# Threshold attention and a gated FFN on one core: the first weights fetched between the first operands, ScalarE's table loaded at once, one unsplit job, and two VectorE operations laid over separate columns

## The chip, the cores and the metric

The kernel runs on one core of one Trainium2 chip. The metric is the device time of one execution in microseconds: the median of the runs shown. Before the change it is 1088.98 us over 3 runs (1088.27 to 1091.62). A core has five engines that run their own instruction streams in order and wait for each other by semaphores: TensorE (PE, with PEld for its weight loads), VectorE (DVE), ScalarE (ACT), GpSimd (POOL) and SyncE (SP), which here issues every DMA.

## The reference

Eight batches, eight heads, 576 positions, head dimension 64. Attention keeps only the scores within tau of their row's maximum. Its output, heads side by side (512 wide), goes through a mixing step with the position before, and then through a feed-forward part with a squared ReLU and a sigmoid gate.

```python
scores = scale * np.matmul(q, k.transpose(0, 1, 3, 2))
thresh = np.max(scores, axis=-1, keepdims=True) - tau
scores = np.where(scores >= thresh, scores, -1000000000.0)
attn = np.exp(scores - np.max(scores, axis=-1, keepdims=True))
attn = attn / (np.sum(attn, axis=-1, keepdims=True) + 1e-09)
x = np.matmul(attn, v)                  # then heads side by side: (8, 576, 512)
x_prev = np.concatenate([np.zeros((B, 1, D)), x[:, :-1, :]], axis=1)
xk = mu_k * x + (1.0 - mu_k) * x_prev
xr = mu_r * x + (1.0 - mu_r) * x_prev
k = np.maximum(xk @ w_k, 0.0)           # w_k: 512 x 1024
v = k * k @ w_v                         # w_v: 1024 x 512
r = 1.0 / (1.0 + np.exp(-(xr @ w_r)))   # w_r: 512 x 512
out = r * v
```

## The kernel before

**Jobs and units.** A job is one pair of heads of one batch. It fetches its operands (`raw`: queries and keys, and `v`), scales the queries on ScalarE (line 427, which needs a factor made from tau by two small VectorE operations, lines 295 and 303), and goes through units of 128 query rows for both heads, and one unit for the last 64 rows. A job is either *plain*, and multiplies the operands as they are (line 530), or *split*: ScalarE rounds them to a high half (line 448), GpSimd subtracts to get the low half (line 458, in two pieces), eight DMAs stack the halves into `st` tiles (line 477), and the scores are products of stacked halves (line 541). The number of plain jobs at the start is `PLAIN`, 2 here.

**The softmax of a unit.** For each head: the maximum (VectorE, line 575), the threshold (ScalarE, line 583), the exponential (ScalarE, line 591), and mask and sum in one (VectorE, line 599). Then, for both heads at once, an addition to the two sums and a reciprocal (VectorE, lines 609 and 610). GpSimd scales the rows (line 624), the TensorE transposes them (line 648), ScalarE or VectorE empties the PSUM (lines 666 and 668), and the TensorE multiplies by the values (line 728). The small numbers of a unit live in `sm`, a tile of 4 kinds by 2 heads, so the two sums lie in neighbouring columns.

**The weights.** All three weight matrices arrive as 64-bit words, in 20 pieces of 128 x 512 (8 of w_k, 4 of w_r, 8 of w_v). Each piece is rebuilt as a 32-bit number in `xT[1]`, which serves as a scratch tile until the second batch needs it: absolute value (ScalarE, line 353), clamp (VectorE, line 361), mask and shift (VectorE, line 375), sign and low bits from the words (VectorE, lines 382 and 392, with two SBUF inputs), then rounding (ScalarE, line 399) and the rest (GpSimd, line 403). So each piece costs the VectorE four operations.

**The feed-forward part.** It runs in chunks of 256 positions: differences (GpSimd, line 821), mixing (VectorE, line 830), rounding and rest (lines 843 and 851), products with w_k (line 873), w_r (line 915) and w_v (line 937).

**What sets the order.** No engine's order is written by hand. Each step is entered with its engine, an assumed duration, its inputs and outputs, and a key; a list scheduler (`Plan.order`) then takes, on each engine, the step that can start first by its own assumed clock, and the lower key among equals. DMAs are one engine of this plan, so the order in which SyncE issues them comes out of it too. A weight's fetch has a key and an earliest time (`wait`); `W0` to `W3` set those times: 3.0 us and then every 3.5 us for the eight pieces of w_k, from 50 us on every 2 us for the other twelve. The order is fixed when the program is built.

Of the kernel before, what the change touches and what calls it, by code (L numbers as in the profile page):

```python
# [8 lines left out]
F32 = mybir.dt.float32  # L9
FR = mybir.dt.float32r  # L10
AF = mybir.ActivationFunctionType
ALU = mybir.AluOpType
# [4 lines left out]
W_MIN = 2.0 ** (0x38 * 2 - 127)  # L17
W_MAX = 2.0 ** (0x8F - 127) * (1 + 0x6FFFFF / 2.0**23)
# [199 lines left out]
def tile_threshold_attention_then_rwkv_ffn(  # L218
# [14 lines left out]
    V, A, G, PE, SY = nc.vector, nc.scalar, nc.gpsimd, nc.tensor, nc.sync  # L233
# [4 lines left out]
    P = 128  # L238
# [22 lines left out]
    add = plan.add  # L261
    DQ = 0.55
    HALF = 2
    W0, W1, W2, W3, AVK = 3.0, 3.5, 50.0, 2.0, 4.5
    PREP, PB, VB, COLD, EARLY = 8, 2, 2, 24, 30
    EV = ("ACT", 0.49), ("DVE", 0.6)
    KMAX, KEXP, KMASK = 0.0, 0.0, 0.5
# [1 line left out]
    def sbuf(tag, shape, dtype=F32, bufs=1):  # L269
        return plan.buf(sb, tag, shape, dtype, bufs)  # L270

    def psum(tag, shape, bufs):
        return plan.buf(ps, tag, shape, F32, bufs)

    def fixed(name, shape, dtype=F32):
        return plan.buf(const, name, shape, dtype, make=lambda: const.tile(shape, dtype, name=name))
# [7 lines left out]
    small = fixed("small", [P, 4])  # L284
# [2 lines left out]
        0.06,  # L287
        lambda: SY.dma_start(small.get()[:, 0:1], tau.rearrange("(o t) -> o t", o=1).broadcast_to([P, 1])),
        writes=[(small, 0)],
        key=-100,  # L290
    )
    add(
        "DVE",
# [2 lines left out]
        reads=[(small, 0)],  # L296
        writes=[(small, 1)],
        key=-100,
# [5 lines left out]
        reads=[(small, 0)],  # L304
        writes=[(small, 2)],
        key=-100,
# [5 lines left out]
    xT = [fixed(f"xT{j}", [P, NCT, SM + 1]) for j in range(2)]  # L312
# [2 lines left out]
    xE = fixed("xE", [P, NCT, NE, ST + 1])  # L315


    bd = fixed("bd", [P, 2, P], FR)
    add("DVE", 0.3, lambda: V.memset(bd.get().bitcast(F32), 0.0), writes=[bd], key=-99)

# [5 lines left out]

    pieces = {}

    def weight(j, name, w, c, f, key, wait):
        plan.soft = True  # L330
        tag = f"w{name}{c}{f}"
        words = sbuf(tag, [P, 512, 2], U32)
        piece = sbuf(tag, [P, 2, 512], FR)
        pieces[name, c, f] = piece
        col = j % 4
        box = (xT[1], (col, 0)), (xT[1], (col, 1))

        def t():
            return xT[1].get()[:, col, 1 : 1 + 512]

        add(
            "DMA",
            DQ,
            lambda: SY.dma_start(words.get().rearrange("p n w -> p (n w)").bitcast(I64), w[c, f]),
            writes=[words],
            key=key - 6,
            kb=512,
            wait=wait,
        )
        add(  # L350
            "ACT",
            0.56,
            lambda: A.activation(t(), words.get()[:, :, 1].bitcast(F32), AF.Abs),
            reads=[words],
            writes=box,
            key=key,
        )
        add(
            "DVE",
            0.55,  # L360
            lambda: V.tensor_scalar(t(), t(), W_MIN, W_MAX, op0=ALU.max, op1=ALU.min),
            writes=box,
            key=key,
        )

        def u():
            return t().bitcast(U32)

        def word(y):
            return words.get()[:, :, y]  # L370

        add(
            "DVE",
            0.55,
            lambda: V.tensor_scalar(u(), u(), 0x07FFFFFF, 3, op0=ALU.bitwise_and, op1=ALU.logical_shift_left),
            writes=box,
            key=key,
        )
        add(
            "DVE",  # L380
            0.85,
            lambda: V.scalar_tensor_tensor(  # L382
                u(), word(1), 0xC0000000, u(), op0=ALU.bitwise_and, op1=ALU.bitwise_or
            ),
            reads=[words],
            writes=box,
            key=key,
        )
        add(
            "DVE",  # L390
            0.85,
            lambda: V.scalar_tensor_tensor(  # L392
                u(), word(0), 29, u(), op0=ALU.logical_shift_right, op1=ALU.bitwise_or
            ),
            reads=[words],
            writes=box,
            key=key,
        )
        add("ACT", 0.53, lambda: A.activation(piece.get()[:, 0], t(), AF.Copy), reads=box, writes=[(piece, 0)], key=key)
        add(  # L400
            "POOL",
            1.27,
            lambda: G.tensor_tensor(piece.get()[:, 1], t(), piece.get()[:, 0].bitcast(F32), op=ALU.subtract),
            reads=[(piece, 0), *box],
            writes=[(piece, 1)],
            key=key,
        )
        plan.soft = False
# [142 lines left out]
    def softmax(unit):  # L551
        n = unit["n"]
        ys = (0, 1) if unit["kind"] == "P" else (1,)

        sm = sbuf("sm", [P, 4, 2], F32, 4)
        p = unit["p"] = sbuf("p", [P, 2, S], F32, PB)
        ss = {y: psum("s", [P, 2, 512], 2) for y in ys}
        scores(unit, ss, float(n))
        for y in ys:
            key = float(n + (y if len(ys) == 2 else 0))  # L560
            s = ss[y]

            def sv(s=s):
                return s.get()[:, :, 0:HS]

            def pv(y=y):
                return p.get()[:, y].rearrange("p (a b) -> p a b", a=2)

            def col(j, y=y):
                return sm.get()[:, j, y : y + 1]  # L570

            add(
                "DVE",
                0.67,
                lambda sv=sv, col=col: V.tensor_reduce(col(0), sv(), axis=AX.XY, op=ALU.max, negate=True),  # L575
                reads=[s],
                writes=[(sm, (0, y))],
                key=key - KMAX,
            )
            add(  # L580
                "ACT",
                0.186,
                lambda col=col: A.activation(col(1), col(0), AF.Identity, bias=small.get()[:, 1:2], scale=-1.0),  # L583
                reads=[(sm, (0, y)), (small, 1)],
                writes=[(sm, (1, y))],
                key=key - KEXP,
            )
            add(
                "ACT",
                0.625,  # L590
                lambda sv=sv, pv=pv, col=col: A.activation(pv(), sv(), AF.Exp, bias=col(0)),  # L591
                reads=[s, (sm, (0, y))],
                writes=[(p, y)],
                key=key - KEXP,
            )
            add(
                "DVE",
                0.74,
                lambda sv=sv, pv=pv, col=col: V.scalar_tensor_tensor(  # L599
                    pv(), sv(), col(1), pv(), op0=ALU.is_ge, op1=ALU.mult, accum_out=col(2)  # L600
                ),
                reads=[s, (sm, (1, y))],
                writes=[(p, y), (sm, (2, y))],
                key=key - KMASK,
            )
        ysl = slice(ys[0], 2)

        def invert():
            V.tensor_scalar(sm.get()[:, 2, ysl], sm.get()[:, 2, ysl], 1e-9, None, op0=ALU.add)  # L609
            V.reciprocal(sm.get()[:, 3, ysl], sm.get()[:, 2, ysl])  # L610

        add(
            "DVE",
            0.33,
            invert,
            reads=[(sm, (2, y)) for y in ys],
            writes=[(sm, (3, y)) for y in ys],
            key=n + 0.5,
        )
        for y in ys:  # L620
            add(
                "POOL",
                0.715,
                lambda y=y: G.tensor_scalar(  # L624
                    p.get()[:, y], p.get()[:, y], sm.get()[:, 3, y : y + 1], 0.0, op0=ALU.mult, op1=ALU.add
                ),
                reads=[(sm, (3, y))],
                writes=[(p, y)],
                key=n - 1.0,
            )  # L630
# [329 lines left out]


    halved = {j: ([0, 1], [2, "T", 3]) for j in range(HALF)}
    PLAIN = 2
    jobs = []
    n = 0
    for b in range(B):
        for part, order in enumerate(halved.get(b, (["T", 0, 1, 2, 3],))):
            for hp in range(NPAIR):
                job = dict(ji=len(jobs), b=b, hp=hp, first=n, groups={}, plain=len(jobs) < PLAIN, units=[])
                job.update(tail="T" in order, tg=int(part == 1), src=qk, nq=S, c0=0)  # L970
# [8 lines left out]
    wlist = [  # L979
        (name, w, c, f)  # L980
        for name, w in (("k", w_k), ("r", w_r), ("v", w_v))
        for f in range(w.shape[1])
        for c in range(w.shape[0])
    ]
    wfr = [W0 + W1 * j if j < 8 else W2 + W3 * (j - 8) for j in range(len(wlist))]
    wat = [2.0 + 2.0 * j for j in range(len(wlist))]

    operands(jobs[0], -1.0)
    add("DMA", DQ, lambda: SY.dma_start(mu_sb.get(), mu.rearrange("p (j c) -> p j c", j=2)), writes=[mu_sb], key=0.0)
    for j, (name, w, c, f) in enumerate(wlist):  # L990
        weight(j, name, w, c, f, wat[j], wfr[j])
    for job in jobs:
        if job["ji"] + 1 < len(jobs):
            operands(jobs[job["ji"] + 1], float(jobs[job["ji"] + 1]["first"]))
        b, seen = job["b"], set()
# [9 lines left out]
        if job["hp"] == NPAIR - 1:  # L1005
            key = unit["n"] - 30.0
# [60 lines left out]
```

## Time and profile before

| what | value |
|---|---|
| median of 3 runs | 1088.98 us |
| the profiled execution | 1088.13 us |
| its span, first to last instruction | 1086.3 us |
| mean granted TensorE clock | 0.986 |
| PE busy | 1019.4 us (94%) |
| DVE busy | 777.1 us (72%) |
| ACT busy | 736.4 us (68%) |
| POOL busy | 581.6 us (54%) |
| chain that ended last, by engine | PE 74%, DVE 15%, ACT 4%, DMA 2% |

The page divides the span into 40 slices of 27 us and shows each engine's busy share in tenths. The shares over the whole span mix two stages, so they are read slice by slice. A group's line gives count, busy time in us, mean duration in ns, and then the engine's idle time before it with what ended it. A matrix product's end is modelled, so a busy TensorE need not be one at its peak.

### The profile page before, as it was taken

The page shows a single profiled execution, that of the slowest core. Times are in us where ns is not written, and L with a number is a line of the kernel's source. Part 1 is how long each engine was busy: PE and PEld are TensorE (multiplying, and loading weights), DVE is VectorE, ACT ScalarE, POOL GpSimd, SP SyncE. Part 2 cuts the span into 40 slices and gives each one's busy share as a digit, 9 for nine tenths or more (in the row PEclk, how much of TensorE's full clock was granted, in tenths as well). Part 3 has the DMA queues.
Part 4 walks back from the last instruction along what each step waited for, and adds up shares of the span by engine and source line. Part 5 has one row for each costly group of instructions (what it writes and reads, how often), then busy time and mean ns, then how long its engine had stood idle before and what let it go on. Part 6 is the DMA issues. An engine that isn't in the chain of part 4 may idle for free.

```text
span 1086.3 us, 19493 instructions
## 1 busy us (share of the span) xinstructions
PE 1019.4 (94%) x6832; PEld 842.7 (78%) x6832; DVE 777.1 (72%) x1707; ACT 736.4 (68%) x1556; POOL 581.6 (54%) x590
## 2 busy tenths in 40 slices
PE   4666899999999999999999999999999999999998
PEld 2444766888888887888887878886889788888887
DVE  6999999779887788777877877766878498222220
ACT  4776876787867777687777767865777667344442
POOL 3666776556645556556455554573555445344441
PEclk8888999999999999999999999999999999999999
DMA  6784467556445344453544434541545041000000
GB/s 217 197 304 108 115 171 188 131 159 182 110 117 127 100 109 113 112 130 96 125 115 104 105 98 114 119 96 50 137 105 128 25 100 35 21 20 20 20 21 19
DMA packets 44351, 118.44 MB, mean 109 GB/s; under 512 B 7392, under 2 KB 10976, under 8 KB 44256
## 3 DMA queue, kind: packets, MB, share of 16 engines
q1 hardware_dynamic: 44256, 117.21, 41.4%
q8 instruction: 55, 0.90, 0.3%
q14 instruction: 40, 0.33, 0.1%
HBM read 46.14 MB, written 9.44 MB: 51 GB/s over the span
## 4 chain that ended last, share of the span: by engine, by line
PE 74%; DVE 15%; ACT 4%; DMA 2%; issue 2%; SPq 1%; POOL 1%; POOLq 0%; ACTq 0%; DVEq 0%
PE w L873 17%; PE w L937 15%; PE w L728 12%; PE s L541 10%; PE w L648 10%; PE w L915 8%; DVE p L599 4%; DVE sm L575 3%; DVE mk L830 2%; PE s L516 2%; ACT p L591 1%; DVE sm L609 1%; DVE xT L392 1%; DVE xT L382 1%; DMA st<-lo 1%
## 5 line engine op out<-in xcount | busy, mean ns | idle before, releaser
L624 POOL TENSOR_SCALAR p<-p,sm 128x576 f32<-128x576 f32 x288 | 226.8, 798 | 222.8 <-DVE sm L610 160.3
L599 DVE SCALAR_TENSOR_TENSOR p<-s,sm,p 128x576 f32<-128x576 f32 x288 | 232.2, 813 | 59.4 <-ACT p L591 55.9
L873 PE MATMUL w<-xk,wk 128*128 128x256 f32 x1728 | 233.8, 284 | 0.0
L575 DVE TENSOR_REDUCE sm<-s 128x1 f32<-128x576 f32 x288 | 210.8, 749 | 31.5 <-PE s L541 21.3
L937 PE MATMUL w<-wv,k 128*128 128x512 f32 x864 | 220.9, 396 | 0.9 <-ACT pm L666 0.9
L648 PE MATMUL w<-ident,p 128*128 128x128 f32 x1312 | 197.0, 282 | 24.9 <-POOL p L624 23.6
L873 PEld LDWEIGHTS w<-xk,wk 128*128 128x128 f32 x1728 | 217.6, 189 | 1.7 <-issue 0.5
L591 ACT ACTIVATE p<-s,sm 128x576 f32<-128x576 f32 x288 | 209.8, 730 | 0.4
L648 PEld LDWEIGHTS w<-ident,p 128*128 128x128 f32 x1312 | 154.0, 144 | 67.1 <-POOL p L624 44.2
L937 PEld LDWEIGHTS w<-wv,k 128*128 128x128 f32 x864 | 155.5, 188 | 28.7 <-ACT pm L666 1.4
L851 POOL TENSOR_TENSOR xk<-mk,xk 128x512 fp32r<-128x512 f32 x72 | 93.2, 1294 | 112.4 <-ACT xk L843 112.2
L583 ACT ACTIVATE sm<-sm,small 128x1 f32<-128x1 f32 x288 | 83.6, 290 | 100.0 <-DVE sm L575 92.9
L666 ACT ACTIVATE pm<-w 128x512 f32<-128x512 f32 x174 | 102.5, 591 | 69.9 <-PE w L648 69.0
L728 PE MATMUL w<-pm,v 128*64 128x256 f32 (+1 forms) x1024 | 142.7, 414 | 2.4 <-DVE pm L668 1.9
L830 DVE SCALAR_TENSOR_TENSOR mk<-m,mu_sb,xT 128x256 f32<-128x256 f32 x128 | 84.1, 697 | 73.0 <-POOL xk L851 73.0
L541 PE MATMUL s<-st 128*128 128x288 f32 x496 | 116.5, 316 | 17.6 <-issue 8.7
L896 POOL TENSOR_TENSOR k<-r,k 128x512 fp32r<-128x512 f32 x72 | 93.7, 1303 | 72.9 <-ACT k L886 69.0
L458 POOL TENSOR_TENSOR lo<-raw,hi 128x576 fp32r<-128x576 f32 (+2 forms) x76 | 106.8, 1422 | 39.9 <-ACT hi L448 38.9
L728 PEld LDWEIGHTS w<-pm,v 128*64 128x64 f32 x1024 | 69.6, 137 | 55.7 <-issue 8.6
L915 PE MATMUL w<-wr,xk 128*128 128x512 f32 x432 | 110.4, 396 | 0.0
L541 PE MATMUL s<-st,st 128*128 128x288 f32 x496 | 109.0, 301 | 0.0
L541 PEld LDWEIGHTS s<-st 128*128 128x128 f32 x496 | 79.6, 191 | 37.6 <-issue 20.4
(62 smaller groups left out, 1125.0 us busy)
## 6 DMA issues: line engine op xcount, KB each, us to landing
raw<-in_qk SPq DMA_DIRECT2D x24, 608.0 KB, 4.8
st<-hi SPq DMA_DIRECT2D x48, 304.0 KB, 3.2
st<-lo SPq DMA_DIRECT2D x48, 304.0 KB, 4.0
v<-in_v SPq DMA_DIRECT2D x40, 320.0 KB, 3.9
out<-sg SPq DMA_DIRECT2D x32, 256.0 KB, 2.0
st<-hi SPq DMA_DIRECT2D x48, 144.0 KB, 3.4
st<-lo SPq DMA_DIRECT2D x48, 144.0 KB, 3.8
wk<-in_w_k SPq DMA_DIRECT2D x8, 512.0 KB, 5.9
```

The source lines that it names most:

```text
L458: lambda cs=cs: G.tensor_tensor(lo.get()[:, cs], raw.get()[:, cs], hi.get()[:, cs].bitcast(F32), op=ALU.subtract),
L541: PE.matmul(ss[y].get()[:, z, 0:HS], l.get()[:, c * P : (c + 1) * P], r.get()[:, keys(y, z)], start=(j == 0), stop=(j == 1),)
L575: lambda sv=sv, col=col: V.tensor_reduce(col(0), sv(), axis=AX.XY, op=ALU.max, negate=True),
L591: lambda sv=sv, pv=pv, col=col: A.activation(pv(), sv(), AF.Exp, bias=col(0)),
L599: lambda sv=sv, pv=pv, col=col: V.scalar_tensor_tensor(pv(), sv(), col(1), pv(), op0=ALU.is_ge, op1=ALU.mult, accum_out=col(2)),
L624: lambda y=y: G.tensor_scalar(p.get()[:, y], p.get()[:, y], sm.get()[:, 3, y : y + 1], 0.0, op0=ALU.mult, op1=ALU.add),
L648: PE.transpose(pt.get()[:, c, :], p.get().rearrange("p y s -> p (y s)")[:, o : o + P], ident.get())
L728: PE.matmul(o.get()[hs, 0:n], vt.get()[:, c, hs], pt[:, 0:n], start=(c == 0), stop=(c == 4))
L830: V.scalar_tensor_tensor(d.get()[:, y, o : o + n], diff.get()[:, y, o : o + n], mu_sb.get()[:, j, hc + y : hc + y + 1], prv[:, hc + y], op ...
L873: PE.matmul(h.get()[:, f], l, r, start=(ct == 0 and i == 0), stop=(ct == NCT - 1 and i == 2))
L915: PE.matmul(z.get(), l, r, start=(ct == 0 and i == 0), stop=(ct == NCT - 1 and i == 2))
L937: PE.matmul(vps.get(), l, r, start=(ft == 0 and i == 0), stop=(ft == NFT - 1 and i == 2))
```

## The change

Six edits. Tau is fetched second, behind the first job's operands. A one-column exponential of a zero is added at ScalarE's start, which brings its table load there. The first two weights are fetched between the first operands, and the fetch times become 1.5 us apart for w_k and 1 us apart for the rest. `PLAIN` is 1. The two one-input operations of the weight conversion go over the same 512 columns in another order: column 0, column 256, column 1, column 257 and so on. And `sm` is turned round, so that the two sums lie four columns apart.

```diff
-    W0, W1, W2, W3, AVK = 3.0, 3.5, 50.0, 2.0, 4.5
+    W0, W1, W2, W3, AVK = 3.0, 1.5, 50.0, 1.0, 4.5
...
         lambda: SY.dma_start(small.get()[:, 0:1], tau.rearrange("(o t) -> o t", o=1).broadcast_to([P, 1])),
         writes=[(small, 0)],
-        key=-100,
+        key=-13.9,
...
+    add(
+        "ACT",
+        1.5,
+        lambda: A.activation(small.get()[:, 3:4], xT[0].get()[:, 0, 0:1], AF.Exp),
+        reads=[(xT[0], "zero")],
+        writes=[(small, 3)],
+        key=-99,
+    )
...
+        def far(x):
+            return x.rearrange("p (a b) -> p b a", a=2)
...
             lambda: SY.dma_start(words.get().rearrange("p n w -> p (n w)").bitcast(I64), w[c, f]),
             writes=[words],
-            key=key - 6,
+            key=fetch,
             kb=512,
-            wait=wait,
+            wait=max(wait, 0.0),
...
-            lambda: V.tensor_scalar(t(), t(), W_MIN, W_MAX, op0=ALU.max, op1=ALU.min),
+            lambda: V.tensor_scalar(far(t()), far(t()), W_MIN, W_MAX, op0=ALU.max, op1=ALU.min),
...
-            lambda: V.tensor_scalar(u(), u(), 0x07FFFFFF, 3, op0=ALU.bitwise_and, op1=ALU.logical_shift_left),
+            lambda: V.tensor_scalar(far(u()), far(u()), 0x07FFFFFF, 3, op0=ALU.bitwise_and, op1=ALU.logical_shift_left),
...
-        sm = sbuf("sm", [P, 4, 2], F32, 4)
+        sm = sbuf("sm", [P, 2, 4], F32, 4)
...
             def col(j, y=y):
-                return sm.get()[:, j, y : y + 1]
+                return sm.get()[:, y, j : j + 1]
...
-            V.tensor_scalar(sm.get()[:, 2, ysl], sm.get()[:, 2, ysl], 1e-9, None, op0=ALU.add)
-            V.reciprocal(sm.get()[:, 3, ysl], sm.get()[:, 2, ysl])
+            V.tensor_scalar(sm.get()[:, ysl, 2], sm.get()[:, ysl, 2], 1e-9, None, op0=ALU.add)
+            V.reciprocal(sm.get()[:, ysl, 3], sm.get()[:, ysl, 2])
...
-    PLAIN = 2
+    PLAIN = 1
...
-    wfr = [W0 + W1 * j if j < 8 else W2 + W3 * (j - 8) for j in range(len(wlist))]
+    wfr = [W0 + W1 * (j - 2) if j < 8 else W2 + W3 * (j - 8) for j in range(len(wlist))]
     wat = [2.0 + 2.0 * j for j in range(len(wlist))]
+    wfe = [-13.0, -8.5, *(w - 6.0 for w in wat[2:])]
...
-        weight(j, name, w, c, f, wat[j], wfr[j])
+        weight(j, name, w, c, f, wat[j], wfe[j], wfr[j])
```

The plan's order comes out differently nearly everywhere, most of all in the first 130 us. Two places follow; line numbers of the changed kernel are 14 higher from line 344 on (16 at the end), and the number behind a tile's name only tells one buffer from another.

The VectorE's first operations before, from the two that prepare tau's factors (line 295) to the first piece of a weight that is taken up (`xT`, with `wk` the words it is made of); `s` are scores, `p` the exponentials:

```order
L303 TENSOR_SCALAR small<-small 128x1
L575 TENSOR_REDUCE sm_103<-s_94 128x1
L575 TENSOR_REDUCE sm_103<-s_96 128x1
L599 SCALAR_TENSOR_TENSOR p_107,sm_103<-s_94,sm_103,p_107 128x576
L599 SCALAR_TENSOR_TENSOR p_107,sm_103<-s_96,sm_103,p_107 128x576
L609 TENSOR_SCALAR sm_103<-sm_103 128x2
L610 RECIPROCAL sm_103<-sm_103 128x2
L361 TENSOR_SCALAR xT_77<-xT_77 128x512
L375 TENSOR_SCALAR xT_77<-xT_77 128x512
```

The same place now:

```order
L303 TENSOR_SCALAR small<-small 128x1
L375 TENSOR_SCALAR xT_75<-xT_75 128x256x2
L389 TENSOR_SCALAR xT_75<-xT_75 128x256x2
L589 TENSOR_REDUCE sm_117<-s_101 128x1
L589 TENSOR_REDUCE sm_117<-s_103 128x1
L396 SCALAR_TENSOR_TENSOR xT_75<-wk_0_82,xT_75 128x512
L613 SCALAR_TENSOR_TENSOR p_125,sm_117<-s_101,sm_117,p_125 128x576
L613 SCALAR_TENSOR_TENSOR p_125,sm_117<-s_103,sm_117,p_125 128x576
L623 TENSOR_SCALAR sm_117<-sm_117 128x2
L624 RECIPROCAL sm_117<-sm_117 128x2
```

Two operations of the first weight stand ahead of the first maximum and a third ahead of the first mask, where before no weight was touched until the first unit's softmax was through.

SyncE's first DMAs before (`small` is tau, `raw` an operand of queries and keys, `v` the values, `wk` a weight):

```order
L288 DMA small<-in_tau 128x1
L419 DMA raw_75<-in_qa 128x896
L419 DMA raw_81<-in_qa 128x896
L436 DMA v_83<-in_v 128x640
L436 DMA v_85<-in_v 128x640
L989 DMA mu_sb<-in_mu 128x8
L344 DMA wk_0_89<-in_w_k 128x512
L344 DMA wk_0_101<-in_w_k 128x512
L344 DMA wk_0_112<-in_w_k 128x512
L344 DMA wk_0_130<-in_w_k 128x512
```

And now:

```order
L433 DMA raw_71<-in_qa 128x896
L288 DMA small<-in_tau 128x1
L358 DMA wk_0_82<-in_w_k 128x512
L433 DMA raw_84<-in_qa 128x896
L358 DMA wk_0_86<-in_w_k 128x512
L450 DMA v_88<-in_v 128x640
L450 DMA v_90<-in_v 128x640
L1005 DMA mu_sb<-in_mu 128x8
L358 DMA wk_0_94<-in_w_k 128x512
L358 DMA wk_0_98<-in_w_k 128x512
```

The first operand passed tau, one weight stands between the two operands and one behind them. Three more weights follow, and only then the first stacked halves, which are those of the second job.

More of the change, by code (lines that the diff above doesn't have):

```diff
@@ L327, in tile_threshold_attention_then_rwkv_ffn, with weight @@
     pieces = {}
-    def weight(j, name, w, c, f, key, wait):
+    def weight(j, name, w, c, f, key, fetch, wait):
         plan.soft = True
@@ L624, in softmax @@
                 lambda y=y: G.tensor_scalar(
-                    p.get()[:, y], p.get()[:, y], sm.get()[:, 3, y : y + 1], 0.0, op0=ALU.mult, op1=ALU.add
+                    p.get()[:, y], p.get()[:, y], sm.get()[:, y, 3:4], 0.0, op0=ALU.mult, op1=ALU.add
                 ),
```

## The prediction

> **What bounds the kernel now.** I read the page's forty slices first, then sums of busy time by stretch, then the groups of the stretch that stood out.
>
> ```profile
> span 1086.3 us, 19493 instructions
> ...
> PE   4666899999999999999999999999999999999998
> ...
> DVE  6999999779887788777877877766878498222220
> ...
> PEclk8888999999999999999999999999999999999999
> ```
>
> One slice is 27 us. From the sixth on the TensorE is busy 90% or more; before that it is not, and there it is the VectorE that shows nines. So there are two stages, and a change of the first 130 us must be priced on the VectorE. The sums by stretch say how hard that bound is (columns: stretch, its length, then PE, PEld, DVE, ACT and POOL busy, granted clock, DMA share):
>
> ```profile
> 0.00:10.00 10.00, 2.29 (x8) 1.19 (x8) 1.03 (x6) 2.19 (x3) 0.70 (x6) 1.00 0.74 265
> 10.00:101.00 91.00, 56.20 (x292) 37.94 (x293) 88.46 (x157) 59.83 (x129) 55.30 (x48) 0.83 0.67 205
> 101.00:163.00 62.00, 56.22 (x367) 43.12 (x367) 57.46 (x119) 52.56 (x113) 46.07 (x44) 1.00 0.56 144
> 163.00:1086.00 923.00, 904.70 (x6169) 760.45 (x6168) 630.19 (x1429) 621.82 (x1312) 479.56 (x493) 1.00 0.38 96
> ```
>
> From 10 to 101 us the VectorE works 88.46 of 91 us while the TensorE idles 34.8. A microsecond of VectorE time saved there is close to a microsecond of the span. From 163 us on the TensorE idles 18.3 of 923, and VectorE time is worth little. The groups of the VectorE in the first 101 us (count, busy us, mean ns):
>
> ```profile
> L361 DVE TENSOR_SCALAR xT<-xT 128x512 f32<-128x512 f32 x15 | 11.6, 790 | 0.0
> L375 DVE TENSOR_SCALAR xT<-xT 128x512 uint32<-128x512 uint32 x14 | 10.5, 758 | 0.0
> L392 DVE SCALAR_TENSOR_TENSOR xT<-wk,xT 128x512 uint32<-128x512 uint32 x8 | 7.8, 970 | 0.0
> L382 DVE SCALAR_TENSOR_TENSOR xT<-wk,xT 128x512 uint32<-128x512 uint32 x8 | 6.4, 805 | 0.0
> L609 DVE TENSOR_SCALAR sm<-sm 128x2 f32<-128x2 f32 x10 | 5.3, 533 | 0.3
> ```
>
> Against these stand the shortest, middle and longest of the same lines (ns):
>
> ```profile
> L361 DVE TENSOR_SCALAR xT<-xT x20: 407/421/1506, 13.3 to 152.8; 128x512 f32<-128x512 f32 x20
> L375 DVE TENSOR_SCALAR xT<-xT x20: 406/693/1748, 13.7 to 155.1; 128x512 uint32<-128x512 uint32 x20
> L392 DVE SCALAR_TENSOR_TENSOR xT<-wk,xT x8: 670/674/2016, 17.5 to 55.0; 128x512 uint32<-128x512 uint32 x8
> ```
>
> So the one-input operations of the weight conversion can take 0.41 us and average 0.76 (22.1 us over 29). The same 512 columns take 0.67 with two inputs: L361 and L375 move two columns a step when nothing holds them. What holds them stands in the order of time:
>
> ```profile
> 12.97 0.17 DVE L609 TENSOR_SCALAR sm<-sm 128x2 f32<-128x2 f32 x1
> ...
> 20.32 0.94 DVE L609 TENSOR_SCALAR sm<-sm 128x2 f32<-128x2 f32 x1
> ```
>
> ```profile
> 19.97 1.26 POOL L403 TENSOR_TENSOR wk<-xT,wk 128x512 fp32r<-128x512 f32 x1 [4.57 <-ACT wk L399]
> ```
>
> The two-column sum took 0.17 us beside an idle GpSimd; at 20.32 it took 0.94 and ended at 21.26, where the GpSimd's operation ended (21.23). Over the whole run the form with one column never shows this:
>
> ```profile
> L609 DVE TENSOR_SCALAR sm<-sm 128x2 f32<-128x2 f32 x128 | 42.0, 328 | 2.1
> L609 DVE TENSOR_SCALAR sm<-sm 128x1 f32<-128x1 f32 x32 | 4.7, 148 | 0.6
> ```
>
> **The change part by part**, against the profiled run's 1088.1 us (span 1086.3). The median of the runs shown, 1088.98, lies 0.9 above it; I add that at the end.
>
> The start. Today ScalarE waits for the first operand and only then loads its table:
>
> ```profile
> 0.74 0.39 SPq L288 DMA_DIRECT2D small<-in_tau  x1
> 1.18 0.90 SPq L419 DMA_DIRECT2D raw<-in_qa  x2
> ...
> 3.92 0.15 DVE L295 TENSOR_SCALAR small<-small 128x1 f32<-128x1 f32 x1 [2.73 <-DMA small<-in_tau]
> ...
> 5.37 1.28 ACT L427 ACT_TABLE_LOAD   x1 [5.37 <-DMA raw<-in_qa]
> 6.66 0.91 ACT L427 ACTIVATE raw<-raw,small 128x256 f32<-128x256 f32 x2
> ...
> 9.55 1.42 DVE L575 TENSOR_REDUCE sm<-s 128x1 f32<-128x576 f32 x2 [5.42 <-PE s L530]
> ```
>
> The load moves under that wait. The operand goes out 0.44 us earlier and lands near 4.9; tau goes out at about 1.2, lands 3.2 later at 4.4, and two small VectorE operations follow. So the first scaling starts near 5.0 and not at 6.66, and the first maximum could start at 7.9. But two conversion operations of the first weight now stand ahead of it. That weight goes out third, at about 1.6:
>
> ```profile
> wk<-in_w_k SPq DMA_DIRECT2D x8, 512.0 KB, 5.9
> ```
>
> The median is in us from issue to landing. ScalarE's part and the first use of the values:
>
> ```profile
> L353 ACT ACTIVATE xT<-wk 128x512 f32<-128x512 f32 x8 | 5.2, 671 | 0.5 <-POOL wk L403 0.5
> ...
> 27.66 1.12 PE L728 MATMUL w<-pm,v 128*64 128x256 f32 x2
> ```
>
> It lands at about 7.5, ScalarE's absolute value takes 0.67, and two operations at 0.67 end at 9.5. The values and mu now go out behind two weights; their first product starts at 27.66 today, so they have time. The maximum starts as late as today, with 1.3 us of conversion already done, and a third operation partly fills a hole before the masks: **-1.5 us** (0 if the weight lands late, since the VectorE waits in order; -3 if all of the 1.6 us is kept too).
>
> Sums on columns apart. If a step of four columns ends the waiting, ten operations fall from 533 to 148 ns: **-3.8** (0 if it does not).
>
> Conversion on columns apart, and with it the main unknown. The trace has no one-input operation whose neighbours in order lie 256 columns apart. Its ends come from the rows: 406 and 670 ns give 264 ns for 256 steps and 142 fixed. If nothing waits and nothing is paid, 0.41 each, -10.3 over 29. If it runs one column a step and the far column costs nothing, 0.67 each: 19.4 us for today's 22.1. If every column costs two steps, 142 + 4 x 264 = 1.20 each, +12.7. I take 0.67, **-2.7**, because the L392 row is the nearest: same columns, same tile, one column a step, and its other operand is already read with every second column skipped at no cost.
>
> Waits that move. L382 and L392 have two inputs from SBUF and wait today (805 and 970 against 670). If L361 and L375 no longer take the wait, the operation behind them meets the same GpSimd. Between nothing and all 10.3 us of today's waits I take 0.1 us for each of the 28 behind the first 101 us's conversions (14 of either line), about as much again as L382 waits today: **+3**.
>
> One unsplit job. The second job now gets a high and a low half: one ScalarE copy, eight more DMAs, and two GpSimd operations of 0.81 and 1.75 us:
>
> ```profile
> L458 POOL TENSOR_TENSOR lo<-raw,hi 128x640 fp32r<-128x640 f32 x4 | 7.0, 1745 | 0.0
> ...
> L458 POOL TENSOR_TENSOR lo<-raw,hi 128x256 fp32r<-128x256 f32 x2 | 1.6, 806 | 0.0
> ```
>
> The VectorE hides it: it reaches that job's first maximum after two units and most of five weights, long after the halves are in. But the 1.75 us run where the first two-input conversion would, which may wait: **+0.5** (0 to +2.6). Its score matrix products sit on an engine that idles there: 0.
>
> Order of the weights. By the fourteenth weight the VectorE has done 22 maxima in both orders, so up to 101 us the VectorE's work is the same. Weights in bursts can delay operands in the one DMA queue; with the VectorE full that costs nothing up to its 2.5 us of idle: 0, with 4 either way.
>
> After 101 us, by the whole run's rows of the conversion and those of the sums above:
>
> ```profile
> L375 DVE TENSOR_SCALAR xT<-xT 128x512 uint32<-128x512 uint32 x20 | 14.3, 723 | 0.0
> L361 DVE TENSOR_SCALAR xT<-xT 128x512 f32<-128x512 f32 x20 | 13.8, 707 | 0.0
> ```
>
> 11 conversions are left in 28.1 - 22.1 = 6.0 us, at 0.67 for a mean of 0.55 (+1.4); of the 118 later two-column sums the waits come to 36.7 - 17.5 = 19 us, nearly all beside a busy TensorE. Together **-1** (-5 to +2).
>
> Sum: -1.5 - 3.8 - 2.7 + 3 + 0.5 - 1 = **-5.5**, so 1082.6 on the profiled run and 1083.5 as a median; its own range, with 4 for the order, is 1078 to 1088.
>
> [...]
>
> **Rivals.**
> - Slower: the far column costs a second step in each conversion. For it: consecutive columns are 1 KiB apart, as in no row here. Against: the skipped columns of L392 cost nothing. At 1.20 us each the 29 give +12.7 and not -2.7: sum +9.9, 1099. If the two columns a step stay as well, 0.67 plus today's wait of 0.36 is 1.03 each, +7.6, with the sums unchanged, -1.5 + 7.6 + 0.5: 1095.6. It decides from a mean of 0.86 us, where -5.5 is used up (2.8 us over 29 above today's 0.76). I put it at 1097, chance 0.27.
> - The step changes nothing: both kinds keep waiting as now. For it: the counts of elements are the same, and only the spacing differs. Left are -1.5 + 0.5: 1088. Chance 0.22.
> - More than forecast: the waits do not move to the two-input operations, and GpSimd, freed as well, shortens the softmax for the TensorE, which waited 19.4 us for it in the first 140 us:
>
> ```profile
> PE w L648 <- POOL p L624: 19.4, 14, 6.7
> ```
>
>   No +3, and -5 for -1 later: -12.5, 1076.5. Chance 0.08.
>
> **How the numbers follow.** Forecast 0.43, 1083.5. The range 1077 to 1097 leaves out the far part of the first rival and of the last. A measurement of this kernel tells about 0.3% (3.3 us) from no change. Faster: 0.34 of the forecast's 0.43, all of the last rival's 0.08, 0.02 of the second: 0.44. Within: 0.08 of the forecast, 0.18 of the second, 0.02 of the first: 0.28. Slower: 0.28.
>
> **What would show it.** The two-column sum's mean falls from 328 to about 150 ns, or stays. The conversion's one-input lines show a shortest time of 0.67 and a mean close to it; 0.41 means that nothing changed, 1.0 or more that the step is paid. L382's successor shows means above 805 if waits moved. The table load starts before 2 us and the first scaling near 5.0. The stretch from 10 us to the fourteenth weight, 91 us now, ends near 95. If the VectorE idles more than 3 us in it, an operand was late and the sum is wrong in its order term.

## The result, and the profile after

| kernel | median | runs | ratio to before (95%) |
|---|---|---|---|
| before, beside it | 1088.80 us | 1088.27 to 1091.62 | 1 |
| changed | 1102.01 us | 1099.62 to 1106.08 | 1.0122 (1.0091 to 1.0153) |

The changed kernel is 1.2% slower, and its time lies beyond the range's upper end of 1097. The profiled execution took 1099.62 us. Its page, with the lines that answer to those of before:

```profile
span 1097.8 us, 19494 instructions
...
PE   3776899999999999999999989999999999999998
...
DVE  6999898776788788888778887855878488322220
...
PEclk9877999999999999999999999999999999999999
```

The TensorE's row differs in the first three slices (3, 7 and 7 where before had 4, 6 and 6) and in the twenty-fourth, 631 to 659 us (8 for 9). The sums by stretch (same columns as before):

```profile
0.00:10.00 10.00, 2.29 (x8) 1.18 (x8) 1.25 (x6) 2.91 (x5) 0.70 (x6) 1.00 0.67 222
10.00:101.00 91.00, 57.44 (x283) 40.03 (x284) 88.04 (x153) 59.96 (x127) 63.00 (x50) 0.83 0.77 223
101.00:163.00 62.00, 53.90 (x344) 42.56 (x344) 56.04 (x110) 48.54 (x104) 44.40 (x38) 0.94 0.46 118
163.00:1097.00 934.00, 911.98 (x6201) 766.98 (x6199) 638.68 (x1441) 625.17 (x1323) 484.27 (x499) 1.00 0.38 96
```

From 10 to 101 us the VectorE is as full as before (88.04 for 88.46) but gets less done: 153 operations for 157. From 101 to 163 us the TensorE works 53.90 us where it had worked 56.22, at 0.94 of the clock and not 1.00. After 163 us the TensorE idles 22.0 us, 18.3 before.

The conversion's one-input lines (shortest, middle, longest in ns) and the sum:

```profile
L375 DVE TENSOR_SCALAR xT<-xT x20: 619/709/1734, 9.3 to 145.6; 128x512 f32<-128x512 f32 x20
L389 DVE TENSOR_SCALAR xT<-xT x20: 630/754/1975, 10.0 to 152.9; 128x512 uint32<-128x512 uint32 x20
```

```profile
L389 DVE TENSOR_SCALAR xT<-xT 128x512 uint32<-128x512 uint32 x20 | 17.8, 923 | 0.1
L375 DVE TENSOR_SCALAR xT<-xT 128x512 f32<-128x512 f32 x20 | 17.0, 873 | 2.7 <-ACT xT L367 2.7
...
L623 DVE TENSOR_SCALAR sm<-sm 128x2 f32<-128x2 f32 x128 | 42.6, 333 | 2.5
```

The sum kept its duration (333 ns, 328 before): a step of four columns ends no wait. (In the first 101 us alone its mean did fall, from 533 to 351 ns. That is the order's doing: in `sm_before`, described below, which has the columns apart in the order of before, the eleven additions of that stretch, one of them on one column, average 499 ns, as they do before.) The conversion went from 407 ns at the shortest to 619, and its longest of 1.7 to 2.0 us shows that the waits stayed too. Over all 40 operations the mean went from 715 to 898 ns: (17.8 + 17.0) for (14.3 + 13.8) us, 6.7 us more VectorE time.

The start (start and duration in us; in brackets the idle time ahead and what ended it):

```profile
0.73 1.28 ACT L321 ACT_TABLE_LOAD   x1 [0.73 <-PEq L1072]
0.74 0.40 SPq L433 DMA_DIRECT2D raw<-in_qa  x1
...
1.19 0.41 SPq L288 DMA_DIRECT2D small<-in_tau  x1
1.65 0.43 SPq L358 DMA_DIRECT2D wk<-in_w_k  x1
...
6.36 0.15 DVE L295 TENSOR_SCALAR small<-small 128x1 f32<-128x1 f32 x1 [5.17 <-DMA small<-in_tau]
...
6.61 0.51 ACT L441 ACTIVATE raw<-raw,small 128x256 f32<-128x256 f32 x1 [4.38 <-DVE small L303]
...
8.61 0.66 ACT L367 ACTIVATE xT<-wk 128x512 f32<-128x512 f32 x1 [1.49 <-DMA wk<-in_w_k]
...
10.52 1.39 DVE L589 TENSOR_REDUCE sm<-s 128x1 f32<-128x576 f32 x2
```

The table loads at once, and nothing comes of it: tau's user starts 5.2 us after tau's issue (3.2 when tau went first), so the first scaling starts at 6.61 as it did at 6.66. The weight is there at 8.6 and not 7.5, and the first maximum, which waits behind two of its operations, starts at 10.52 for 9.55.

### The profile page after: what moved, and what is told of

Its sections match the earlier page's. It is cut to its first block, busy times and chain, and to the rows that moved or that the text cites. A ratio compares the mean times of both kernels' runs of the same rounds, so it can differ in the third digit from the quotient of the medians.

```text
span 1097.8 us, 19494 instructions
## 1 busy us (share of the span) xinstructions
PE 1025.6 (93%) x6832; PEld 850.8 (77%) x6832; DVE 784.0 (71%) x1707; ACT 736.6 (67%) x1558; POOL 592.4 (54%) x592
## 4 chain that ended last, share of the span: by engine, by line
PE 72%; DVE 15%; ACT 6%; POOL 3%; issue 2%; DMA 1%; SPq 0%; POOLq 0%; ACTq 0%
PE w L887 16%; PE w L951 16%; PE w L742 12%; PE w L662 11%; PE s L555 10%; PE w L929 7%; DVE p L613 4%; DVE sm L589 3%; DVE mk L844 3%; POOL p L638 2%; ACT p L605 2%; PE s L530 2%; DVE sm L623 1%; DVE xT L375 1%; DVE xT L396 1%
## 5 line engine op out<-in xcount | busy, mean ns | idle before, releaser
L638 POOL TENSOR_SCALAR p<-p,sm 128x576 f32<-128x576 f32 x288 | 230.3, 810 | 214.5 <-DVE sm L624 159.9
L887 PE MATMUL w<-xk,wk 128*128 128x256 f32 x1728 | 238.6, 287 | 1.0 <-DVE sg L957 0.9
L887 PEld LDWEIGHTS w<-xk,wk 128*128 128x128 f32 x1728 | 220.6, 191 | 2.6 <-DVE sg L957 1.2
L472 POOL TENSOR_TENSOR lo<-raw,hi 128x576 fp32r<-128x576 f32 (+2 forms) x78 | 109.2, 1417 | 47.5 <-ACT hi L462 39.9
L555 PE MATMUL s<-st 128*128 128x288 f32 x504 | 118.7, 317 | 14.2 <-DVE p L613 7.1
L555 PE MATMUL s<-st,st 128*128 128x288 f32 x504 | 112.0, 304 | 0.0
L555 PEld LDWEIGHTS s<-st 128*128 128x128 f32 x504 | 81.9, 192 | 34.9 <-issue 26.2
```

Of the source, the lines that this page charges most:

```text
L472: lambda cs=cs: G.tensor_tensor(lo.get()[:, cs], raw.get()[:, cs], hi.get()[:, cs].bitcast(F32), op=ALU.subtract),
L555: PE.matmul(ss[y].get()[:, z, 0:HS], l.get()[:, c * P : (c + 1) * P], r.get()[:, keys(y, z)], start=(j == 0), stop=(j == 1),)
L638: lambda y=y: G.tensor_scalar(p.get()[:, y], p.get()[:, y], sm.get()[:, y, 3:4], 0.0, op0=ALU.mult, op1=ALU.add),
L887: PE.matmul(h.get()[:, f], l, r, start=(ct == 0 and i == 0), stop=(ct == NCT - 1 and i == 2))
```

## The experiments

For each kernel I also worked out its **lag**: matrix products are counted backward from the end, each at its usual duration, and for the same amount left the kernel's time is compared with before's. It says where in the run a difference arises. Lags are from single profiled executions, so a microsecond of theirs is noise; in kernels with another order the columns 293 and 453 also move by some 3 us with the durations that are put for the products. The column "end" is the last product. In us, at the points that before reaches at these times:

| kernel | 123 | 293 | 453 | 614 | 773 | end |
|---|---|---|---|---|---|---|
| changed | +5.4 | +5.2 | +5.7 | +2.3 | +10.7 | +11.1 |
| `lay_before` | +6.3 | +6.4 | +6.1 | +7.9 | +7.9 | +7.8 |
| `far_before` | +7.2 | +7.1 | +6.8 | +7.0 | +7.0 | +7.1 |
| `ord_after` | -1.5 | -2.6 | -2.6 | -6.1 | +2.2 | +2.5 |
| `nofar_after` | -2.2 | -1.2 | -1.2 | -4.7 | +5.1 | +5.4 |
| `plain_after` | +6.3 | +8.7 | +9.0 | +4.2 | +7.3 | +7.6 |
| `fetch_after` | +1.6 | +1.4 | +5.3 | +5.4 | +3.9 | +4.3 |
| `tau_after` | +2.9 | +3.1 | +3.1 | -0.4 | +7.9 | +8.2 |
| `move_ord` | +0.4 | +0.8 | +0.8 | -2.7 | +4.4 | +4.7 |
| `late_after` | +11.3 | +11.4 | +13.1 | +11.7 | +15.4 | +16.7 |
| `split_before` | -1.6 | -2.3 | -3.9 | -5.7 | -6.8 | -7.2 |

**Layouts or order.** `lay_before` is the kernel before with both layouts, which move no instruction; `ord_after` is the changed kernel with both undone.

```diff
-            lambda: V.tensor_scalar(t(), t(), W_MIN, W_MAX, op0=ALU.max, op1=ALU.min),
+            lambda: V.tensor_scalar(far(t()), far(t()), W_MIN, W_MAX, op0=ALU.max, op1=ALU.min),
...
-        sm = sbuf("sm", [P, 4, 2], F32, 4)
+        sm = sbuf("sm", [P, 2, 4], F32, 4)
```

> The kernel before with the two layouts alone (sums four columns apart, conversion over far columns); every engine's order is that of before. Theory L (the far step's price on the VectorE makes the loss): the conversion's one-input lines go from 0.71 to about 0.90 us each, 40 x 0.19 = 7.5 us, most of it before 101 us where the VectorE is full: 1094 to 1097 us. Theory O (the new order of the plan makes the loss, most of it after 280 us): only the 2 to 3 us by which the changed kernel is late at the fourteenth weight: 1090.5 to 1092. Both: the two-column sum's mean stays near 330 ns.

> The changed kernel with both layouts undone; its order, table load, fetches and one unsplit job stay. Theory L: near the kernel before or under it, 1087 to 1091 us. Theory O: 3 us under the changed kernel at most, 1097 to 1101 us, with the late stretches after 280 us and at 640 us still there.

`lay_before` 1093.29 us, 1.0040 (1.0024 to 1.0055), and `ord_after` 1091.88 us, 1.0030 (1.0018 to 1.0042). Neither theory holds alone: each half costs some 3 to 4 us. Each layout by itself, and the sums' layout in the changed order:

> The kernel before with the conversion's columns apart alone; every engine's order stays that of before. Theory L (the far column of the conversion costs, the sums' layout costs nothing): 1092 to 1095, the same as with both layouts (1093.3); the shortest L365 and L379 near 0.62 us, the two-column sum at 320 to 335 ns. Theory S (the two layouts share the cost): 1090 to 1091.5. Theory O (only the order costs): 1089.

> The kernel before with the sums on columns apart alone. Theory L: 1088 to 1090, the two-column sum at 320 to 335 ns as before, since a step of four columns changes nothing. Theory S: 1090 to 1091.5, and then a VectorE row on sm, or GpSimd's scaling row that reads a column of it, is longer than before. The prediction's reading (a step ends the waiting): 1085, the sum near 150 ns.

> The changed kernel with the conversion's columns beside one another again, the sums still apart. If the layouts and the order add up: 1101 - 4.4 = 1096.6. If the conversion's far column meets the changed order worse than that of before (the weights come in bursts, and the weights' products wait for the last conversion): 1091 to 1093, as with neither layout (1091.9). If the sums' layout is what meets the order badly: 1099 to 1101.

`far_before` 1094.97, 1.0038 (1.0021 to 1.0055), its runs from 1091.42 to 1096.69; `sm_before` 1088.37, 0.9990 (0.9982 to 0.9999); `nofar_after` 1091.97, 1.0031 (1.0020 to 1.0042). All of the layouts' price is the conversion's. In the changed order that price is higher by medians: `nofar_after` is 2.5 us slower than before and the changed kernel, which has the conversion's columns apart besides, 13.2. That makes 10.7 us for the one edit, where it costs 5.5 in the order of before. So the second expectation for `nofar_after` came out, by its range. But its reason is not shown, and the profiled runs show no more than 5.7 us for it (7.1 in the order of before). `far_before` shows it with no instruction moved:

```profile
L365 DVE TENSOR_SCALAR xT<-xT x20: 606/705/1771, 13.1 to 159.9; 128x512 f32<-128x512 f32 x20
L379 DVE TENSOR_SCALAR xT<-xT x20: 598/720/1929, 13.8 to 162.5; 128x512 uint32<-128x512 uint32 x20
```

Its 7 us are all there by 123 us and stay to the end: the stage that the VectorE bounds pays them, the rest gives nothing back. In `sm_before` the sum is the old one:

```profile
L609 DVE TENSOR_SCALAR sm<-sm 128x2 f32<-128x2 f32 x128 | 42.0, 328 | 2.2
```

**What the sum's wait is worth.** If the step does not end it, two additions on one column each do; and the addition can be left out.

```diff
-            V.tensor_scalar(sm.get()[:, 2, ysl], sm.get()[:, 2, ysl], 1e-9, None, op0=ALU.add)
+            for y in range(ysl.start, 2):
+                V.tensor_scalar(sm.get()[:, 2, y : y + 1], sm.get()[:, 2, y : y + 1], 1e-9, None, op0=ALU.add)
```

> The kernel before with the addition on the sums' two columns written as two additions on one column each, which the trace shows at 146 ns and without waits. If the wait of the two-column sum beside GpSimd was worth what the prediction says: ten of 0.53 us in the first 101 us become twice 0.15, -2.3 us, so 1086 to 1087.5. If the wait only moves to the next VectorE operation (two-input operations and the maxima): 1088 to 1090. [...]

> The kernel before without the addition of 1e-9 to the sums (left out; a sum that holds the maximum's exponential is at least 1, where 1e-9 is below the last bit). Against the kernel with two one-column additions (1080.7) it saves 288 of 0.147 us and their issue, 42 us of VectorE time. If VectorE time beside a busy TensorE is worth a tenth of itself or so, as -8.7 for about 11 us less VectorE time and its waits suggests: 1075 to 1079. If only the wait with its place in the chain from sum to GpSimd counted: 1079 to 1081.

> The changed kernel with the addition on two sums written as two additions on one column each. If the two-column sum's waits cost as much here as in the order of before (-8.7 us): 1091 to 1094. If the conversion with columns apart, which holds the VectorE longer, now takes the waits that the sums leave: 1096 to 1100.

`split_before` 1080.74, 0.9917 (0.9904 to 0.9931); `drop_before` 1076.50, 0.9879 (0.9863 to 0.9894); `split_after` 1093.39, 1.0034 (1.0022 to 1.0045), so 8.6 us below the changed kernel by medians. `split_before` gained more than any of its theories gave; the other two, put down when it was known, came out as their first theories say. The VectorE at the place that the prediction quotes, 20.32 us, behind the sum before and then in `split_before`:

```profile
21.30 0.17 DVE L610 RECIPROCAL sm<-sm 128x2 f32<-128x2 f32 x1
21.38 0.67 DVE L392 SCALAR_TENSOR_TENSOR xT<-wk,xT 128x512 uint32<-128x512 uint32 x1
```

```profile
20.24 0.27 DVE L610 TENSOR_SCALAR sm<-sm 128x1 f32<-128x1 f32 x2
20.54 0.17 DVE L611 RECIPROCAL sm<-sm 128x2 f32<-128x2 f32 x1
20.62 1.19 DVE L392 SCALAR_TENSOR_TENSOR xT<-wk,xT 128x512 uint32<-128x512 uint32 x1
```

And GpSimd's scaling behind that reciprocal, before and then in `split_before`:

```profile
21.56 1.35 POOL L624 TENSOR_SCALAR p<-p,sm 128x576 f32<-128x576 f32 x1 [0.33 <-DVE sm L610]
```

```profile
21.24 1.44 POOL L625 TENSOR_SCALAR p<-p,sm 128x576 f32<-128x576 f32 x1
```

Here the wait is not gone, it has moved: the conversion behind the reciprocal takes 1.19 us for 0.67. In the first 101 us most of it moves so: the sums fall from 5.5 to 2.7 us, the weights' four VectorE operations rise from 48.1 to 50.2. Over the whole run it does not: the sums fall from 46.7 to 35.1 us, the conversion rises by 2.6, and the VectorE is busy 11 us less. And the reciprocal now runs at 20.54 and not at 21.30, ahead of the wait, so GpSimd no longer idles for it. The lag says where that is worth most: 1.6 us by 123, and 5.6 of the 7.2 from there on, where the TensorE is busy 98%. Its waits after 163 us, before and then in `split_before` (line waited at, releaser, us in total, times, longest):

```profile
PE s L541 <- DVE p L599: 5.0, 9, 1.8
PE w L648 <- POOL p L624: 3.6, 7, 1.0
```

```profile
PE s L541 <- DVE p L599: 3.7, 6, 1.9
...
PE w L649 <- POOL p L625: 1.3, 3, 0.6
```

These two explain 3.6 us of the 5.6; the rest is not traced to a place. VectorE time as such is worth less than a wait in this chain: `drop_before` takes another 26 us of busy time from the VectorE (765.9 to 739.7) and 4.2 us from the run, where `split_before` gains 8.7 us for 11.

**The start.** `start_before` puts the exponential alone into the kernel before, `tau_after` puts tau's transfer first again in the changed one. Both leave every other step where it was.

```diff
+    plan.out.insert(plan.out.index(zero) + 1, len(plan.steps) - 1)
...
+    plan.out.remove(first)
+    plan.out.insert(0, first)
```

> The kernel before with one step put in by hand: ScalarE's small exponential, and so its table load, behind the first memset. tau stays the first transfer and no other step moves. The prediction's term with tau in time: table load before 2 us, first scaling near 5.4 (when the operand lands) instead of 6.66, first maximum near 8.3 instead of 9.55, and 0.5 to 1.5 us off the time: 1087.5 to 1089. If the start is bound by something else (the first operand's scaling as a whole, the VectorE's work up to 101 us being the same): 1088.5 to 1090, with the first maximum earlier and the VectorE idle for as much longer behind it.

> The changed kernel with tau's transfer put first again by hand and nothing else moved. If tau's late landing (5.2 us after its issue, behind an operand and beside a weight) is what kept the first scaling at 6.6: it starts near 5.4, and 0.5 to 1.5 us come off: 1099.5 to 1101.5. If the weights beside the first operand delay that too: scaling still past 6 and no change (1100.5 to 1102.5).

`start_before` 1088.83, 0.9984 (0.9975 to 0.9993): the first scaling starts at 5.33 and 1 us stays off to the end. `tau_after` 1097.85, 1.0076 (1.0064 to 1.0089), 4 us below the changed kernel by medians (2.9 by the profiled runs) and more than expected:

```profile
3.93 0.15 DVE L295 TENSOR_SCALAR small<-small 128x1 f32<-128x1 f32 x1 [2.75 <-DMA small<-in_tau]
...
5.32 0.51 ACT L441 ACTIVATE raw<-raw,small 128x256 f32<-128x256 f32 x1 [3.09 <-DMA raw<-in_qa]
...
6.53 0.67 ACT L367 ACTIVATE xT<-wk 128x512 f32<-128x512 f32 x1 [0.70 <-DMA wk<-in_w_k]
...
8.43 1.38 DVE L589 TENSOR_REDUCE sm<-s 128x1 f32<-128x576 f32 x2
```

With tau ahead of it the weight, issued at the same 1.65 us, is used at 6.53 and not at 8.61, and the first maximum starts 2.1 us earlier. A small transfer behind a large one was late itself, and what came after it was late too. It is tau's place and not the weights between the operands: `fetch_after` (below) has no weight there, and tau's user still starts 5.6 us after the issue.

**The fetch times and the unsplit job**, each put back alone in the changed kernel (the fetch times with their first two weights; `PLAIN` at 2):

> The changed kernel with the weights' keys and fetch times of before; table load, tau's place, layouts and one unsplit job stay. If the early fetches cost (tau behind a weight in the queue, first maximum at 10.5 instead of 9.6 us): about 1 us under the changed kernel at the start. Theory O in its strong form: again several us either way that arise after 163 us.

> The changed kernel with two unsplit jobs again; the plan's order comes out anew. If the split of the second job costs (a low half on GpSimd beside the first conversions, eight more DMAs): 2 to 4 us under the changed kernel in the first 101 us. Theory O in its strong form (any change of the plan's input gives another order of the middle, by chance): a shift of several us either way that the first 101 us don't show.

1092.82, 1.0038 (1.0024 to 1.0053), and 1095.76, 1.0062 (1.0049 to 1.0075). Either alone takes 6 to 9 us off, together more than the order's whole price of 3.0 us, so these are not prices of the parts: each gives another order of the whole run, and the lags diverge where no edit points (at 453 us +5.3 and +9.0).

**The middle of the run.** The changed order is level or ahead up to 614 us and then loses 8 to 10 us by 773, with either layout. There the granted clock falls too:

```profile
640.00:650.00 10.00, 8.08 (x41) 6.12 (x38) 8.49 (x22) 5.33 (x12) 5.55 (x6) 0.83 0.72 188
```

and the TensorE waits twice (from the changed kernel's order of time):

```profile
633.30 2.66 DVE L844 SCALAR_TENSOR_TENSOR mk<-m,mu_sb,xE 128x64 f32<-128x64 f32 x8 [0.67 <-POOL xk L865]
...
636.58 1.18 PE L662 MATMUL w<-ident,p 128*128 128x128 f32 x9 [2.27 <-DVE xE L682]
...
638.32 1.22 ACT L462 ACTIVATE hi<-raw 128x1216 fp32r<-128x1216 f32 x1 [0.26 <-PE s L530]
...
644.64 0.53 PE L555 MATMUL s<-st 128*128 128x288 f32 x2 [1.92 <-issue]
```

First for a copy that stands behind eight mixing operations, for which the plan counts 1.6 us and which take 2.66. Then for the next job's operand: from ScalarE's high half to the first use of `st` there are 6.3 us, which the chain through GpSimd and the queue needs (the first low half goes out at 641.05 and lands at 644.37). Before has 12.5 us at the like place:

```profile
625.22 1.22 ACT L448 ACTIVATE hi<-raw 128x1216 fp32r<-128x1216 f32 x1 [1.36 <-PE s L516]
...
637.72 0.53 PE L541 MATMUL s<-st 128*128 128x288 f32 x2 [0.19 <-DVE p L599]
```

Two waits of 4.2 us, and half the clock for 3.4 us (0.83 over 10 us), make about 5.9 of the 8.4. `move_ord` takes the first wait away from `ord_after`: the mixing operations go behind the two copies. `late_after` and `late_before` alter one planner number that counts from 200 us on.

```diff
+    plan.out.remove(mk)
+    plan.out.insert(plan.out.index(moved) + 1, mk)
...
-    HOP, LATE, FROM = 0.05, 0.3, 200.0
+    HOP, LATE, FROM = 0.05, 0.35, 200.0
```

> The order of the changed kernel with both layouts of before (1091.9), and one VectorE step moved by hand: the eight 64-column mixing operations that stand ahead of the two copies for which the TensorE waits 2.28 us near 628 us now stand behind them. If that place makes the loss of the middle: the wait of 2.3 us is gone, the granted clock stays full near 637 us, the lag against before grows by 2 to 5 us between 610 and 650 us instead of by 8, and the time falls by 2 to 5 us, to 1087 to 1090. If the loss only moves on (the second wait of 1.9 us, for an operand, grows by as much): 1091 to 1092.5 with the clock's drop still there.

> The changed kernel with one number of the planner altered that only counts from 200 us on (the lateness that it allows for transposes, 0.35 for 0.3), so that the first 200 us keep their order. If the 8 us that the changed kernel loses between 285 and 725 us belong to its order there, which no edit of the change aims at: the lag against before stays at 1 to 6 us up to 200 and then goes another way, 1092 to 1098 or above 1104. If that loss follows from the start (operands or buffers late since then): 1099 to 1103 with the same jump near 640.

> The kernel before with the planner's lateness at 0.35 for 0.3, which moves steps only from 200 us on. If an order's price is an accident of its places (the prediction's term: 0 with 4 either way): within 4 us of before, and more likely above than below, 1088 to 1093, with the lag arising in one or two stretches where the TensorE waits over 1.5 us. If the orders are worth the same: 1088.5 to 1090.5.

`move_ord` 1092.64, 1.0032 (1.0020 to 1.0044): nothing gained. The first wait is gone and the second has grown from 1.93 us to 2.56, and the products behind it are slow again (a pair takes 0.68 us at 640.35 and 0.42 at 647.27; in the changed kernel a pair at 646.72 takes 0.68, where the clock is at half):

```profile
638.36 0.50 PE L555 MATMUL s<-st 128*128 128x288 f32 x2 [2.56 <-issue]
```

So the first wait covered only part of the loss. The trace points at the operand that is prepared close to its use; no run here prepares it earlier, so that this is the bound stays argued. `late_after` 1101.67, 1.0110 (1.0094 to 1.0126): the loss between 614 and 773 shrinks to 3.7 us in its profile, yet the time does not fall; its profiled run (1105.2) had lost 11 us in the start already. It settles nothing. `late_before` 1088.02, 0.9989 (0.9980 to 0.9998): 1 us faster with every later step shuffled, its lag between -1.8 and +1.3 on the way.

**A faster kernel.** `drop_before` with the early table load:

> The kernel before without the addition of 1e-9 to the sums (left out; 1076.5 alone) and with ScalarE's small exponential at the start (alone -1.0). If the two add up: 1075 to 1076; if the start's microsecond is lost again in the VectorE's first 100 us: 1076 to 1077.

1075.39 us, 0.9872 (0.9858 to 0.9885), 1.3% faster than before and 2.4% than the changed kernel. The sums are at least 1, so the addition that it leaves out changes nothing in 32 bits. Who wants to keep it writes it on one column at a time, as `split_before` does, for 8.7 us of the gain.

## Why the prediction was wrong

- **What bounds the kernel**: right for the first 101 us, where the VectorE is full: in `far_before` the conversion's one-input lines take 8.3 us more, its two-input lines 2.2 less, and the lag is 7.2. "From 163 us on ... VectorE time is worth little" holds for busy time, but was taken for waits too, and there it failed. The sum's wait sits in the chain to GpSimd's scaling and the TensorE's transposes, and 5.6 us came from there once the reciprocal was ahead of the wait. The share of idle TensorE time bounds the gain at 18 us; it did not say that the gain is nil.
- **Sums on columns apart, -3.8**: the step that failed is "If a step of four columns ends the waiting". It does not: 333 ns for 328, and `sm_before` gives about -1 us. The wait was mis-sized as well: removed from its place by `split_before` it is worth 8.7 us, but only 1.6 of them by 123 us, where 3.8 were put, since there it moves onto the conversion; the larger part lies behind, where the prediction left some 2.4 in its -1.
- **Conversion on columns apart, -2.7**: the step that failed is the choice of 0.67 us each by the two-input row, which counted one column a step and the far column as free. The shortest, 619 ns, is below that row's 670 and 0.21 us above the 407 of before, with the waits on top: 0.91 us in the mean of the first 101 us, past the 0.86 that I had named as the turning point. That is the first rival's second form ("If the two columns a step stay as well"), with a smaller price for the hop: 0.183 us more over 40 operations, where 0.27 over 29 was put. Its sum, 1095.6, is close to `far_before` (1094.97) partly by luck: it counts -1.5 for a start and +0.5 for an unsplit job that `far_before` does not have.
- **Waits that move, +3**: had no object, since the waits did not leave the conversion. The two-input lines take 39.8 us in all in the changed kernel, 37.8 in `far_before` and 40.0 before. The sign that was named, means above 805 ns in L382's successor, did appear (935 ns), but it comes with the order: `ord_after`, whose conversion has neighbouring columns, shows 1084. That waits can move is shown by `split_before`, from the sum onto the conversion.
- **The start, -1.5**: tau's landing "3.2 later" was read from a transfer that went first. Second, it took 5.2, and the weight 1.1 longer than put. The table load alone is worth 1 us (`start_before`); tau's place costs 4 by medians (`tau_after`), which turns the term to about +3.
- **Unsplit job +0.5 and order 0 ± 4**: not separable, as `plain_after` and `fetch_after` show. Together with the start they are worth +3.0 (`ord_after`), inside the 4. But I looked for it only up to 101 us, where that order is ahead; it loses at 614 to 773, where the trace shows one operand prepared 6.3 us before its use, and a clock that falls behind the TensorE's waits (0.83 over 10 us).
- **The range** held each of these alone. It failed since the first rival and a bad order came together, which I had kept apart as cases; their sum was never put down. Step by step, by medians, the order costs 3.0 us (`ord_after`), the sums' layout nothing (`nofar_after`, 2.5 in all), and the conversion's layout the other 10.7 of the 13.2. Layouts priced in the order of before (4.4) and the order (3.0) make only 7.4, so some 6 us come from the two together. The profiled runs do add up (7.1 + 5.4 for 11.1 in the lags). `far_before` was 1095.2 in its profiled run and as low as 1091.4 in others; why it scatters so, and the medians' 6 us, stay open.

## What to carry to other kernels

When an operation waits for another engine, ask first what stands behind it in the chain: two one-column additions of 147 ns each beat one of 328, even where the wait only moved on, since the reciprocal was then ahead of it. A layout that is meant to change how an engine reads should be tried on one line before it is put on forty operations; the shortest duration of the line (407 or 619 ns) tells at once. And a plan's inputs are not local: each edit of them here gave another order 600 us later, so the rivals of an order term have to cover the whole run, and be added to the others.

## What was unexpected of the hardware

- A one-column transfer behind a large one took 4.6 to 5.8 us from issue to use in the eight profiles that have it second, 3.1 to 3.2 in four where it is first (before, `start_before`, `drop_before`, `tau_after`), and in the changed kernel a weight issued behind it was used 2 us later than in `tau_after` (8.61 for 6.53).
- Columns 256 apart cost a one-input VectorE operation 0.21 us at the shortest (619 ns for 407), which is still less than the 670 of a two-input operation on 512 columns, and did not end its waiting beside GpSimd (1.98 us from 83.84 us on, while two GpSimd operations ran from 82.60 to 85.31). By an estimate from these durations, with the prediction's 142 ns fixed and two columns a step, a step takes (619 - 142) / 256 = 1.9 ns where neighbours take (407 - 142) / 256 = 1.0.
- In the changed kernel the granted clock was at half from 645.0 us on, for at least 3.4 us, behind waits of the TensorE of 2.27 and 1.92 us; over 10 us it was 0.83 there, and in `ord_after` and `nofar_after`, with the same order, it was 0.84. In `move_ord`, whose products are slow at the like place, one wait of 2.56 us stood ahead of them. A single wait of 1.94 us near 604 us left the clock full in the profiled run of before (1.00 from 600 to 620 us). What else the clock follows was not shown.
